# A DeltaNet and MLP-mixer kernel on one core: its steps issued in another order

## The chip, the cores and the metric

The kernel runs on 1 core of one Trainium2 chip. A core has a matrix engine (PE, with its weight loads shown apart as PEld), a vector engine (DVE), a scalar engine (ACT), GpSimd (POOL) and a queue that issues DMAs (SP). Each works through its own instructions strictly in the order in which the program issued them, and waits on semaphores for the others. The metric is device microseconds of one execution.

## The reference, cut to what matters

```python
# q, k, v: (4, 8, 768, 48)    beta: (4, 8, 768)
k_n = k / (np.linalg.norm(k, axis=-1, keepdims=True) + 1e-06)
for t in range(S):                                 # a state of 48x48 per batch and head
    y[:, :, t] = np.einsum('bhd,bhde->bhe', q[:, :, t], state)
    v_old = np.einsum('bhde,bhd->bhe', state, kt)
    state = state + bt * np.einsum('bhd,bhe->bhde', kt, vt - v_old)
x = y.transpose(0, 2, 1, 3).reshape(4, 768, 384)
h = np.maximum(xt @ w_tok1, 0.0) @ w_tok2          # over tokens: xt is x transposed, 768 -> 256 -> 768
u = x + h.transpose(0, 2, 1)
out = u + np.maximum(u @ w_ch1, 0.0) @ w_ch2       # over channels, 384 -> 1536 -> 384
```

The mixer's weights come in as 64-bit floats; everything else is 32-bit.

## The kernel before

**Work and its pieces.** The sequence is cut into 24 units of 128 tokens (6 per batch) and 48 chunks of 64 tokens. The recurrence is done chunk by chunk: each unit first needs small Gram matrices of its keys and queries and the inverse of a triangular matrix, and then a chain of 36 chunk steps carries the state on. After that come the token mixing of each batch and its channel mixing, which is most of the matrix work.

Every piece is a Python generator that issues a few instructions at each step. The letters used below: `k` loads keys and queries of a unit, `v` its values; `p` (`prep`, L528) takes squares and norms of the keys (ACT L539, DVE L542, ACT L547 and L548), transposes keys and queries on PE (L562, L582; copied out by ACT L566, L587) and scales a mask and the keys on DVE or POOL (L574, L592); `c` and `d` (`grams`) make the Gram matrices (PE L511, DVE L517); `t` hands them to `i` (`invert`, L717), which inverts a round of four units (two in the second) on DVE; `f`, `h` and `j` put the inverted blocks together (PE L777, L790, ACT L795, L869 and L818); `r` (`recur`, L903) is one chunk step; `w` rounds a piece of the mixer's weights; `m0` and `m1` are the mixer of batches 0 and 1, whose matmuls need no new data of the recurrence for long stretches and stand wherever the order puts them; `T2`, `T3`, `A`, `F` and `B` are token and channel mixing of batches 2 and 3, done by fast matrix products that trade matmuls for additions on DVE (L1296 in `T3`, L1451 and L1478 in `A`, L1578 in `B`); `x`, `z`, `Y` are matmuls on zeros that keep PE busy.

**What sets the order.** One string lists all 2610 steps, word by word (`p0*5` is five steps of `p0`). A loop calls the generators in that order:

```python
for word in order.split():
    name, _, n = word.partition("*")
    for _ in range(int(n or 1)):
        next(jobs[name])
```

There is no other scheduler: the place of a step in the string is its place in the queue of each engine that it uses, the DMA queue among them. Buffers are waited for as they come free.

**A weight piece** (`round_weights`, L271) is a DMA of 384 KB or 256 KB into one of three buffers named `d64` (L280), two conversions on ACT (L286, L287), a shift on DVE (L289) and an addition on POOL (L293), which reads the buffer last. So a load of one piece cannot start before the POOL addition of the piece three loads earlier is done. The four parts are up to four steps of the string, and may stand far apart.

**A chunk step** `r` has one copy on ACT in its middle: `p_w` is made on PE (L944), ACT copies it to `rw_t` (L950), and PE goes on from it (L958, L959) to the next state. ACT's queue holds those copies among the conversions of weights and all other copies.

**The first round** `i0` is a chain on DVE: a transpose (L731), 14 pairs of a product and a sum on one array (L739, L744), and a transpose back (L753); ACT, DVE and PE take over from it, and the recurrence of units 0 to 3 waits for them.

Of the kernel before, what the change touches and what calls it, by code (L numbers as in the profile page):

```python
# [23 lines left out]
def kernel(  # L24
# [41 lines left out]
    B, H, S, D = q.shape  # L66
# [117 lines left out]
    t11 = const.tile([128, NB, HB], FP32, name="t11")  # L184
# [17 lines left out]
    w1 = const.tile([128, NCH, DTOK], FP32, name="w1")  # L202
    w2 = const.tile([128, NDH, S], FP32, name="w2")
# [407 lines left out]
    t16 = spare[:, cuts[1] : cuts[2]].rearrange("s (q t b) -> s q t b", q=2, t=QB)  # L611
# [1173 lines left out]
    p6*2 t5 j1 t5*2 r1*2 j1 j2 p7 h3*2 r1*3 p6*3 i1*2 r2*5 k8*2 f3*2 w9 k9*3 j1*2
    v2*2 i1*3 j2*2 r2*2 f3 i1*2 p6*3 w16 v2 w16*3 r2*2 h3 r2 i1 d6 r3*5 i1*2 w9*3
    v2 d6 h3 v2 w0 h3*2 r3 h3 d6*2 w0 d6 j3 c6*5 r3*4 w0 j2 w0 p8*2 j2 r4 p8 r4*4
    k9*3 j3*2 r4*2 i1*2 w24 i1*2 p7*7 r4 c7 r4 r5*5 k10 p9 k10 p9 c7 r4 c7*3 i1
    w5*2 p7 r5*2 w24*3 r5*3 j3*2 i1 r6*4 w26 v3*5 p9 k11 r6 d7*5 w26*3 p8*3 t6*2
    r6*2 w5*2 p8*4 v4*2 t6 i1 r6*3 h5*2 h4*2 k10*2 f4*3 c8*2 k10 p10 w28*2 c8*2 r7  # L1790
    c8 r7*3 d8*4 p9 d8 w28 h4*5 p9 t6 r7*2 j4 w28 p9*3 r7*2 p9 w7 d9 w7 v4*2 f5*2
    w27*2 w7*2 d9*4 c9*2 f5 c9*3 t7*2 t8 r7*2 t7*2 j4*2 v4 p10*2 h5 r8*3 w29 t8*3
    w29 w27*2 r8*2 w29*2 q3 w29 j4*2 r8 w22*4 t9*3 r8*3 p9 r9 p10 r9*3 t9 v5 h5*3
    j5 i2 r9 w4*2 r8 h5 i2*5 w4 i2 w19*2 k10 w32 p10*2 w32 v7 k12 m0*2 k11 k12 q0
    v5*3 p10*2 r9*2 j5*2 k11*3 i2*2 r9 w4 i2 j5 i2*3 p10 v5 r9*2 d10*3 r10 v7*2 j5
    i2*2 r10*4 w12 i2 k12 i2*2 m0 w32 k11 k12 w32 r10*2 m0 p11 k12*4 w19 p11 r10
    c10 r10 c10 r10 w33 d10*2 q2 Y r11*4 v7 r11*3 w19 c10 q1 w30 c10 r11 k12*2
    i2*3 r11 v6*4 i2*5 m0*3 i2*5 q5 i2 m0 p11*4 c10 p11 m0 p11*2 m0*2 k12*2 w12
    m0*3 v6 f6*3 w12 d11 c11*2 d11*2 c11 w33 c11 d11*2 j6 p12 w12 m0 w33 w30*3
    p12*2 f7*3 j6*2 m0 c11 j7 f6 f8 w27*2 f8 j7 f8 w15 f7 m0 w29 w33 w29 j7 r12*4  # L1800
    w31 j8 p11 t10*3 r12 Y r12 f9 j8 f9 w21 p12 r12 f8 r13*2 w15*2 r12 w15 r13*3
    w31*3 Y r13*2 w33 j8 w21 m0 r13 q4 p12*4 r13*2 m0*2 r14 c12 f9 j9 r14*2 w21
    t10 w20*2 v7 r14*2 c12*2 w33 c12 r14 v8 c12*2 r14*2 w25*2 j9 r14 r15 v8 w21
    r14 r15 w25 r15*3 w25 k13*4 w20 k13*4 p13 k13*2 w20 v8*3 m0*2 p13 w25 p13 m0
    r15 p13 r15 p13 w27 w25 k13*2 j9 m0*4 p13 f9 w23 t12*3 p13 t12 w25 r15*3 c13*6
    w23 k14*7 r16*5 m0 p13 m0*3 w23*4 k14 r16*2 t11 t13*2 j9*2 t11*3 w33 p14 r16*2
    p14*2 w31 m0*3 w31 m0 w31 m0 w23 r17*2 r16 t13 r17 t13 r17*2 p14*2 m0*2 p14 i3
    k14*4 i3*3 k15 v9*2 m0*3 v10 i3*5 k15 i3 r17 k15*2 p14 k15*3 m0 v10*2 i3 k15*2
    m0*2 k15*2 i3*4 r17*4 k15 i3*2 p14 m0*2 i3*6 m0*4 r18 i3 r18*2 v9*3 r18*2 i3*8
    m0*10 v10*2 m0 r18 c14*4 r18*2 m0*2 f10 c14 f10*2 f12*2 p15*3 m0*4 r18 r19 r18  # L1810
    r19*3 j10 f10 j10*2 f12 p15 f11*4 f12 r19 c14 r19 v11 p15*3 k16*7 j11 m0*2
    r19*4 j11 j12 r20*3 k16*2 r20 m0 r20 k16*3 v11 m0 j11 r20*2 v11*2 p15 c15*2
    p10 r20*2 c15 r20 c15*3 f13*3 p16 r21*5 m0 r21*2 p16*4 k17*7 p16 j12*2 p16 k17
    r21*3 m0*3 r22 c16 r22*3 k17*4 v11 r22 c16*4 r22*2 m0 r22 t14 p17 f13 c16 t14
    j13*2 t14 r22 r23 t15*2 t16 r23*2 r22 r23 m0*3 r23 t15*2 r23 p17*5 t16 p17 j13
    t16*2 m0*3 t14 c17*5 r23*2 c17 t17*2 m0*8 p17 t17*2 i4*3 v12 m0 k18 v15*2 i4
    m0 i4 m0 i4*3 m0 i4 k18*2 j13 p16 m0*2 j13 i4*4 m0 v12*3 k18*4 v12 k18 r24*2
    r23 v13*5 m0 k18*4 v15*2 i4*2 m0*2 p18 i4 p18 r24*3 m0 r24 i4 m0 p18*2 r25*4
    p18 k19*8 i4 m1 r25 i4 m1*4 i4 m1 v14 i4*2 v14 i4*8 r24*3 r25*2 m1 v14 i4*2
    v14*2 p18*2 r25 m1*2 p19 m1*5 k19*4 p19 f14*2 r25*5 c18*5 f14 c18 p18 r26*3  # L1820
# [62 lines left out]
```

## Time and profile before

| | |
|---|---|
| median of 3 runs | 624.91 us (623.32 to 626.13) |
| profiled execution: span | 619.7 us, 20909 instructions |
| around the span, median less span | 5.2 us |
| busy: PE | 590.3 us (95%), 8733 instructions |
| busy: DVE | 469.1 us (76%) |
| busy: ACT | 256.9 us (41%) |
| busy: POOL | 109.9 us (18%) |

The profiled execution is listed by its span only; its own time is taken as the median, so that 5.2 us of the time lie outside the span. The span runs from the first instruction to the last. Busy time of PE counts matmuls at whatever clock was granted to the engine at the time, so that a matmul takes twice as long in a stretch of half clock. The profile has for each line of the program, engine and shape the mean time of one instruction, and for each idle stretch of an engine what ended it. A DVE or POOL row that runs into the next one (starts plus times overlap by some hundredths of a microsecond) is read as back to back.

### The profile page before, as it was taken

The numbers are of one execution on the slowest core, as the hardware profiler recorded it, in microseconds if no ns is written. First come the engines' busy times: TensorE is split into PE (matmuls) and PEld (weight loads), VectorE is DVE, ScalarE is ACT, GpSimd is POOL, SyncE is SP. The second block draws the span as 40 slices with busy tenths as digits, with TensorE's granted clock in tenths as the row PEclk, the third lists the DMA queues.
The fourth block names the chain that finished last, engine by engine and source line by source line (L and its number), as shares of the span: only waits on it lengthen the run. The fifth ranks groups of instructions, "written<-read, shape, count | busy, mean of one in ns | idle before, by whom it ended". The sixth has DMA issues, their size and how long they took to land.

```text
span 619.7 us, 20909 instructions
## 1 busy us (share of the span) xinstructions
PE 590.3 (95%) x8733; PEld 515.9 (83%) x8733; DVE 469.1 (76%) x1160; ACT 256.9 (41%) x682; POOL 109.9 (18%) x150
## 2 busy tenths in 40 slices
PE   8588997999999999999999999999999999999998
PEld 5467875667898988877889888897699999999997
DVE  5987875986889855697566996866888898685874
ACT  8758796448521344223551215415352331414200
POOL 2348264225311122003020120010000000000000
PEclk9878797999999999999999999999999999999999
DMA  9667567667653254454445443135102012020001
GB/s 219 136 135 169 138 142 185 129 155 179 126 114 72 67 116 83 95 113 99 92 87 126 83 95 83 32 66 140 32 2 39 1 21 47 12 52 13 14 26 51
DMA packets 154605, 55.52 MB, mean 90 GB/s; under 512 B 129648, under 2 KB 148976, under 8 KB 154512
## 3 DMA queue, kind: packets, MB, share of 16 engines
q1 hardware_dynamic: 154512, 54.20, 39.1%
q8 instruction: 68, 1.11, 0.8%
q14 instruction: 25, 0.20, 0.1%
HBM read 41.19 MB, written 11.21 MB: 85 GB/s over the span
## 4 chain that ended last, share of the span: by engine, by line
PE 74%; DVE 9%; DMA 4%; ACT 4%; issue 2%; SPq 1%; POOL 1%; DVEq 0%; POOLq 0%; ACTq 0%
PE p_c L1668 13%; PE p_r L1498 13%; PE p_o L1689 10%; PE p_a L1570 7%; PE p_b L1570 6%; PE p_g L511 3%; DMA d<-in_moe_w_ch_dram 3%; PE p_h L1608 3%; DVE sub L739 2%; PE p L1593 2%; DVE x L744 2%; PE p_k L920 2%; PE p L1223 1%; PE p_h L1238 1%; PE p_y L1034 1%
## 5 line engine op out<-in xcount | busy, mean ns | idle before, releaser
L1668 PE MATMUL p_c<-u_t,wc 128*128 128x256 f32 x432 | 101.6, 386 | 0.5 <-issue 0.5
L1668 PEld LDWEIGHTS p_c<-u_t,wc 128*128 128x128 f32 x432 | 79.6, 190 | 11.9 <-issue 1.1
L1689 PE MATMUL p_o<-wc,r 128*128 128x192 f32 x360 | 64.6, 331 | 0.7 <-DVE xb L1628 0.7
L739 DVE TENSOR_TENSOR sub<-x 128x84 f32<-128x84 f32 (+24 forms) x178 | 58.4, 328 | 7.4 <-DMA x<-n_dram 2.8
L744 DVE TENSOR_TENSOR x<-x,sub 128x84 f32<-128x84 f32 (+24 forms) x178 | 58.2, 327 | 6.1
L1689 PEld LDWEIGHTS p_o<-wc,r 128*128 128x128 f32 x360 | 58.4, 190 | 2.3 <-DVE xb L1628 1.3
L1677 ACT ACTIVATE r<-p_c 128x512 f32<-128x512 f32 x36 | 21.4, 596 | 51.2 <-PE p_c L1668 46.1
L511 PE MATMUL p_g<-kq 48*64 48x128 f32 (+1 forms) x704 | 34.9, 283 | 4.0 <-ACT kq L587 3.3
L517 DVE TENSOR_TENSOR gm<-p_g,mb 128x512 f32<-128x512 f32 x44 | 28.9, 683 | 8.1 <-PE p_g L511 7.5
L484 POOL TENSOR_TENSOR v_st<-v_st,nrm 128x384 f32<-128x384 f32 x12 | 10.3, 856 | 131.9 <-DMA v_st<-in_v_dram 104.4
L574 POOL TENSOR_TENSOR mb<-mask_c,cs 128x512 f32<-128x512 f32 x20 | 21.2, 1062 | 67.8 <-DVE cs L552 36.9
L511 PEld LDWEIGHTS p_g<-kq 48*64 48x64 f32 (+1 forms) x704 | 26.5, 137 | 7.6 <-ACT kq L587 4.3
L293 POOL TENSOR_TENSOR wc<-w_f,d 128x384 uint32<-128x384 uint32 x24 | 24.6, 1029 | 42.8 <-ACT d L287 14.1
L1511 DVE TENSOR_TENSOR kq<-kq,p_r 128x384 f32<-128x384 f32 x40 | 21.0, 551 | 10.7 <-PE p_r L1498 8.8
L1498 PE MATMUL p_r<-t_d,wc 128*128 128x192 f32 x160 | 28.8, 326 | 0.0
L1511 DVE TENSOR_TENSOR gm<-gm,p_r 128x384 f32<-128x384 f32 x40 | 21.1, 551 | 8.1 <-PE p_r L1498 5.8
L400 DVE STREAM_TRANSPOSE kq<-pads 128x512 f32<-128x512 f32 x24 | 25.5, 1108 | 2.0 <-PE p_w L1038 1.6
L1498 PEld LDWEIGHTS p_r<-t_d,wc 128*128 128x128 f32 x160 | 26.5, 190 | 0.0
L1689 PE MATMUL p_o<-wc,s 128*128 128x192 f32 x144 | 25.7, 330 | 0.6 <-DVE xb L1628 0.6
L1498 PE MATMUL p_r<-pads,wc 128*128 128x192 f32 x128 | 25.4, 326 | 0.0
L1628 DVE TENSOR_TENSOR xb<-xb,p_o 128x192 f32<-128x192 f32 x42 | 14.6, 348 | 13.0 <-PE p_o L1689 12.6
L1689 PEld LDWEIGHTS p_o<-wc,s 128*128 128x128 f32 x144 | 23.3, 190 | 1.2 <-DVE xb L1628 0.9
(315 smaller groups left out, 1387.1 us busy)
## 6 DMA issues: line engine op xcount, KB each, us to landing
d<-in_moe_w_ch_dram SPq DMA_DIRECT2D x24, 384.0 KB, 4.2
v_st<-in_v_dram SPq DMA_DIRECT2D x96, 48.0 KB, 2.9
out_dram<-xb SPq DMA_DIRECT2D x23, 192.0 KB, 2.1
kst<-in_k_dram SPq DMA_DIRECT2D x64, 48.0 KB, 2.8
n_dram<-gm SPq DMA_DIRECT2D x72, 32.0 KB, 2.3
pads<-in_k_dram SPq DMA_DIRECT2D x24, 96.0 KB, 2.9
pads<-in_q_dram SPq DMA_DIRECT2D x24, 96.0 KB, 2.7
gm<-w_dram SPq DMA_DIRECT2D x72, 32.0 KB, 2.3
```

The lines of the kernel that those rows point to most:

```text
L293: nc.gpsimd.tensor_tensor(out=dst.bitcast(U32), in0=f, in1=lo, op=ALU.add)
L400: nc.vector.transpose(kq_of[p // 2][:, i, :, p % 2].rearrange("f p (s g) -> f p g s", g=G), rows_of[i].rearrange("s p (g d) -> s p g d", g ...
L511: nc.tensor.matmul(p_g[PAR[i ^ cc ^ swap(u)], p], kqt[f, p, cc, 0], kqt[f, p, cc])
L517: nc.vector.tensor_tensor(out=blocks(gm_of(u))[:, :, cc, D:GW].rearrange("s p (two n) -> s p two n", two=2), in0=p_g, in1=made[u][:, :, cc ...
L739: nc.vector.tensor_tensor(out=tmp, in0=y[:, :, 0:s, s : s + 1].to_broadcast([n, k, s, w]), in1=y[:, :, s : s + 1, s + 1 : m].to_broadcast( ...
L744: nc.vector.tensor_tensor(out=y[:, :, 0:s, s + 1 : m], in0=y[:, :, 0:s, s + 1 : m], in1=tmp, op=ALU.add,)
L1498: nc.tensor.matmul(p[:, i], pieces[q // width][:, at : at + 128], f[f"u{n}"], start=first and i == 0, stop=True, skip_group_check=True,)
L1511: nc.vector.tensor_tensor(out=o, in0=o, in1=p, op=op_of(sign))
L1570: nc.tensor.matmul(p, a[:, i], w[:, i // 2, i % 2], start=first and i == 0, stop=True, skip_group_check=True,)
L1668: nc.tensor.matmul(p_c[:, k], piece_of(wc1, cb, f * 128)[:, f * 128 : (f + 1) * 128], u_t[:, cb], start=(cb == 0), stop=(cb == NCB - 1),)
L1677: nc.scalar.activation(r2[:, m], p_c, ACTF.Relu)
L1689: nc.tensor.matmul(p, a[:, m], wc2[:, m, j], start=(start and i == 0), stop=(i == NM - 1), skip_group_check=True,)
```

## The change

Only the string is replaced. Both strings have the same 2610 steps, each generator's steps come in their own sequence as before, and both kernels issue the same 4437 matmuls and the same instructions on every other engine; only the order in each queue differs. The first two lines of it:

```diff
     order = """
-    w10 x*4 z w10*2 z w1*4 k1*3 z k1*3 z b p1 z p1 k0*6 p0*2 b*2 p1 w2 p0*5 p1*2
-    w10 p0*2 z w3 w2 c0*3 p0 w3*2 d0*2 w3 c0 p1 c0 d0*3 k2*3 v1 p1*2 w18 k2*2 p1*2
...
+    w10*2 k1*4 w1 b x k1*2 x*2 p1*2 x*3 z w1 k0*3 z w1*2 z w10 k0 w10 z k0*2 w2 z
+    p0 p1 b*2 k3 v1 p0*3 p1*2 z p0*5 d0*5 w2 c0 k2*2 v1*2 v0 p1 c0*4 k2 p0 p1*2
...
```

Two rows of queues tell more than the string does. A row is the line, the operation, output<-inputs by tile name, the shape and how many stand in a row.

**Start of the program, POOL.** This is POOL's queue from the transposed first parts (L679) to the first block handed back (L706 `wc_120<-r_124`), which comes after the DVE chain of `i0`. Before:

```order
L293 TENSOR_TENSOR wc_119<-w_f,d_282 128x384
L574 TENSOR_TENSOR mb<-mask_c,cs 128x512
L293 TENSOR_TENSOR wc_119<-w_f,d_403 128x384
L652 MEMSET r_124 128x32x16
L619 MEMSET z_571 128x2304
L592 TENSOR_TENSOR gm<-kst_98,cs 128x8x48
L706 COPY wc_120<-r_124 32x8x32
```

and now, beginning one instruction before the mask of unit 3 (`mb`, L574):

```order
L679 COPY r_124<-gm 32x8x32 x2
L574 TENSOR_TENSOR mb<-mask_c,cs 128x512
L293 TENSOR_TENSOR wc_119<-w_f,d_301 128x384
L592 TENSOR_TENSOR gm<-kst_98,cs 128x8x48
L293 TENSOR_TENSOR wc_119<-w_f,d_459 128x384
L652 MEMSET r_124 128x32x16
L619 MEMSET z_588 128x2304
L457 TENSOR_TENSOR nrm<-nrm,eps 128x8
L460 TENSOR_TENSOR v_st<-v_st,nrm 128x384
L706 COPY wc_120<-r_124 32x8x32
```

Between the mask and L706 there were one weight addition (L293), two memsets and one scaling of keys (L592). Now there are two weight additions and the same scaling, the memsets, and two instructions of `v` (L457, L460); the scaling stands ahead of the second addition instead of behind both memsets.

**Steps r8 and r9, ACT.** This is ACT's queue around the copy `rw_t<-p_w` of chunk step `r8` (the first L950 in each piece) and of `r9` (the last row). L286 and L287 on `d_...` are the conversions of one weight piece. Before:

```order
L950 COPY rw_t<-p_w 128x192
L795 COPY gm<-p_x 16x8x16 x3
L286 ACTIVATE d_1927<-d_1927 128x256
L287 ACTIVATE d_1927<-d_1927 128x256
L972 ACTIVATE xb<-p_y 64x4x48 x2
L795 COPY gm<-p_x 16x8x16
L286 ACTIVATE d_1954<-d_1954 128x384
L287 ACTIVATE d_1954<-d_1954 128x384
L566 COPY kq<-p_t 128x4x128
L286 ACTIVATE d_1960<-d_1960 128x384
L287 ACTIVATE d_1960<-d_1960 128x384
L950 COPY rw_t<-p_w 128x192
```

and now:

```order
L950 COPY rw_t<-p_w 128x192
L547 ACTIVATE nrm<-ksum 128x8
L548 ACTIVATE ksum<-nrm,eps 128x8
L795 COPY gm<-p_x 16x8x16 x3
L286 ACTIVATE d_1783<-d_1783 128x384
L287 ACTIVATE d_1783<-d_1783 128x384
L972 ACTIVATE xb<-p_y 64x4x48 x2
L286 ACTIVATE d_1965<-d_1965 128x256
L287 ACTIVATE d_1965<-d_1965 128x256
L869 COPY zst<-p_z 32x256 x2
L566 COPY kq<-p_t 128x4x128
L950 COPY rw_t<-p_w 128x192
```

Between the two copies stood three weight pieces (`d_1927`, `d_1954`, `d_1960`); now there are two (`d_1783`, `d_1965`). In front of the copy of `r8` stands, counted from the start of the program, the twenty-first piece instead of the twenty-second (its conversions are the rows right ahead of the copy in both kernels), and in front of that of `r9` the twenty-third instead of the twenty-fifth.

**Token mixing of batch 3, DVE.** This is DVE's queue in the stretch where `T3` ends (L1296 `xb<-xb,p_h`, which frees the results `p_h` of PE's L1372) while `A1` prepares the channel mixing of its second half (L1451, L1478). Before:

```order
L1296 TENSOR_TENSOR xb<-xb,p_h 128x2x192 x8
L1578 TENSOR_TENSOR xb<-xb,p_a 128x192 x2
L1296 TENSOR_TENSOR xb<-xb,p_h 128x192 x4
L1478 TENSOR_TENSOR t_d<-pads 128x192 x3
L1478 TENSOR_TENSOR t_d<-t_d,pads 128x192
L1478 TENSOR_TENSOR t_d<-pads 128x192
L1478 TENSOR_TENSOR t_d<-t_d,pads 128x192
L1296 TENSOR_TENSOR xb<-xb,p_h 128x192 x4
L1478 TENSOR_TENSOR pads<-pads 128x192
```

and now:

```order
L1578 TENSOR_TENSOR xb<-xb,p_a 128x192
L1296 TENSOR_TENSOR xb<-xb,p_h 128x2x192 x8
L1451 STREAM_TRANSPOSE r_6709<-xb 128x3x128
L1478 TENSOR_TENSOR t_d<-pads 128x192 x2
L1578 TENSOR_TENSOR xb<-xb,p_a 128x192
L1296 TENSOR_TENSOR xb<-xb,p_h 128x192
L1478 TENSOR_TENSOR t_d<-pads 128x192
L1478 TENSOR_TENSOR t_d<-t_d,pads 128x192
L1478 TENSOR_TENSOR t_d<-pads 128x192
L1478 TENSOR_TENSOR t_d<-t_d,pads 128x192
L1478 TENSOR_TENSOR pads<-pads 128x192
L1478 TENSOR_TENSOR t_d<-pads,t_d 128x192
```

On PE, four matmuls `p_a` (L1570, `B0`) stood between the last `p_h` of this stretch and the first `p_r`. Now they stand ahead of the last `p_h`, and on DVE a transpose (L1451) and eight additions of `A1` (L1478) have moved in front of or between the additions that free `p_h`.

149 lines of the change are left out of this document (81 added, 68 removed).

## The prediction

> **What bounds the kernel now.** I read the page first: the busy shares, the slices and the chain that ended last.
>
> ```profile
> span 619.7 us, 20909 instructions
> PE 590.3 (95%) x8733; PEld 515.9 (83%) x8733; DVE 469.1 (76%) x1160; ACT 256.9 (41%) x682; POOL 109.9 (18%) x150
> PE   8588997999999999999999999999999999999998
> PEclk9878797999999999999999999999999999999999
> PE 74%; DVE 9%; DMA 4%; ACT 4%; issue 2%; SPq 1%; POOL 1%; DVEq 0%; POOLq 0%; ACTq 0%
> ```
>
> PE is the bound, and an order cannot shorten its matmuls. It can only take away PE's idle time and its stretches of reduced clock. Both lie in the first eighth of the slices. A table by stage says how much there is; its columns are the stretch, its length, busy time of PE, PEld, DVE, ACT and POOL, the granted clock, DMA share and GB/s.
>
> ```profile
> 26.73:40.82 14.09, 8.79 (x44) 4.91 (x45) 12.34 (x36) 4.48 (x9) 6.40 (x6) 0.64 0.79 178
> 98.34:112.56 14.22, 10.61 (x158) 7.47 (x158) 8.86 (x30) 6.74 (x18) 4.82 (x6) 0.64 0.68 173
> 115.65:446.00 330.35, 325.11 (x5602) 271.22 (x5603) 247.03 (x633) 122.31 (x353) 57.35 (x75) 1.00 0.45 100
> 446.00:616.80 170.80, 170.56 (x1045) 169.12 (x1043) 132.84 (x294) 48.34 (x102) 0.00 (x0) 1.00 0.11 24
> ```
>
> From 115.65 us on PE idles 330.35 − 325.11 = 5.2 us and then 170.80 − 170.56 = 0.2 us. So a better order can win little there and only lose, while of the first 115 us the two stretches above alone hold 5.3 and 3.6 us of idle PE, at a clock of 0.64. The third view is what PE waited for from 17 to 115 us (total, times, longest):
>
> ```profile
> PE p_t L582 <- DMA pads<-in_q_dram: 5.4, 1, 5.4
> PE p_s L958 <- ACT rw_t L950: 3.5, 5, 2.0
> PE p_g L511 <- ACT kq L587: 3.3, 4, 1.4
> ```
>
> The first is one wait in the first round's chain, the second the copy in the middle of a chunk step. I went on to the chain and the timelines around these two places, then to the end of the token mixing.
>
> **The change, first place: weights on ACT (85 to 113 us).** The chain of waits runs over loads of weight pieces there. The last such piece of it (start, length) and rows of ACT's timeline (in brackets the idle time before and what ended it):
>
> ```profile
> 104.29 7.29 DMA d<-in_moe_w_ch_dram
> 101.02 0.55 ACT L286 ACTIVATE d<-d 128x384 f32<-128x384 f32 x1 [1.93 <-DMA d<-in_moe_w_ch_dram]
> 102.05 0.32 ACT L950 COPY rw_t<-p_w 128x192 f32<-128x192 f32 x1
> 106.94 0.44 ACT L286 ACTIVATE d<-d 128x256 f32<-128x256 f32 x1 [3.88 <-DMA d<-in_moe_w_tok_dram]
> 107.27 0.42 ACT L287 ACTIVATE d<-d 128x256 uint32<-128x256 uint32 x1
> 108.64 0.55 ACT L286 ACTIVATE d<-d 128x384 f32<-128x384 f32 x1
> 109.66 0.59 ACT L566 COPY kq<-p_t 128x512 f32<-128x512 f32 x1
> 111.67 0.56 ACT L286 ACTIVATE d<-d 128x384 f32<-128x384 f32 x1 [1.42 <-DMA d<-in_moe_w_ch_dram]
> 112.56 0.30 ACT L950 COPY rw_t<-p_w 128x192 f32<-128x192 f32 x1
> 112.89 0.36 ACT L869 COPY zst<-p_z 32x256 f32<-32x256 f32 x1
> ```
>
> ACT, which is idle more than half of the time, stands still for 1.93 + 3.88 + 1.42 = 7.23 us because the next instruction in its queue is a conversion whose load has not landed. Behind those conversions stand the copies of `r8` (102.05) and `r9` (112.56), and the next state waits for these. The new order puts one piece fewer ahead of the first and two fewer ahead of the second. The last one ahead of the copy of `r9` is then a load of 256 KB, as the one converted at 106.94 is now. If it lands when that does, the conversions end at 107.27 + 0.42 = 107.69, and after two copies L869 (0.36 each) and one L566 (0.59) the copy of `r9` comes at 109.0, 3.6 us earlier than 112.56. If it lands only as the second piece does now (108.64), the copy comes at 108.64 + 0.44 + 0.42 + 0.72 + 0.59 = 110.8, 1.8 us earlier. I take 3.6, which is also the idle PE time of this stretch (14.22 − 10.61): a load of this size is the nearest row.
>
> Bounds: nothing, if the loads land later by as much as the copies move up. On SP's queue the load of that piece still stands behind L733, the fetch of the second round, and behind one load that is converted after it; and a buffer is free only when the POOL addition three pieces before is done. On the other side 7.4 us, if the low clock of this stretch goes too: 10.61 × (1 − 0.64) = 3.8 more. So −3.6, from 0 to −7.4.
>
> **Second place: the first round (26 to 41 us).** DVE, POOL, ACT and PE timelines, in that order:
>
> ```profile
> 26.73 1.95 DVE L731 STREAM_TRANSPOSE x<-r 128x1024 f32<-128x1024 f32 x1
> 28.93 0.19 DVE L744 TENSOR_TENSOR x<-x,sub 128x28 f32<-128x28 f32 x1
> 36.39 1.06 DVE L744 TENSOR_TENSOR x<-x,sub 128x28 f32<-128x28 f32 x1
> 37.80 0.71 DVE L753 STREAM_TRANSPOSE r<-x 128x512 f32<-128x512 f32 x1
> 41.20 0.54 DVE L542 TENSOR_REDUCE ksum<-ksq 128x8 f32<-128x384 f32 x1
> 46.42 1.29 DVE L592 TENSOR_TENSOR gm<-lent,cs 128x384 f32<-128x384 f32 x1
> 27.75 1.04 POOL L574 TENSOR_TENSOR mb<-mask_c,cs 128x512 f32<-128x512 f32 x1
> 36.38 1.01 POOL L293 TENSOR_TENSOR wc<-w_f,d 128x384 uint32<-128x384 uint32 x1 [7.59 <-issue]
> 41.77 0.21 ACT L547 ACTIVATE nrm<-ksum 128x8 f32<-128x8 f32 x1
> 42.22 0.60 ACT L781 ACTIVATE z<-p_z,sides 128x128 f32<-128x128 f32 x2
> 30.31 1.09 PE L582 MATMUL p_t<-ident,pads 128*128 128x128 f32 x4 [5.38 <-DMA pads<-in_q_dram]
> 40.82 2.06 PE L777 MATMUL p_z<-r,wc 64*64 64x32 f32 x64 [1.05 <-DVE gm L517]
> ```
>
> PE's longest wait, 5.38 us, ends at 30.31. The new order issues that load of queries right behind the keys of the same unit, so the wait should shrink or go. I cost this at 0: what hides it is DVE's chain from 26.73 to L753, without which p_z (40.82) cannot start. Were that cover gone, it would be worth up to 5.4 us, but nothing in the order shortens that chain.
>
> The chain itself gets longer. DVE has one more L542 inside it (0.54), and a scaling of keys L592 that ran at 46.42 now stands ahead of L731; its 1.29 there overlaps a POOL addition, so I take the 0.54 of L542, which passes over as many elements. Together +1.08. L547 with its partner, which stood ahead of L781 on ACT (42.22 − 41.77 = 0.45), goes earlier: −0.45.
>
> Then POOL. At 36.39 a sum L744 of 28 elements took 1.06 us, at 28.93 the same one 0.19; beside it ran a POOL addition, and both ended together. So a POOL instruction that begins in the chain holds up one sum by about 0.87; beside the transpose L731 the POOL mask at 27.75 did no visible harm. Two or three POOL instructions more (L592 and weight additions) now stand in that part of POOL's queue, where it idled for 7.59 us before. I take one more collision, +0.87, since the first of them can still fall beside L731, which lasts 1.95. [...]
>
> The place: 1.08 − 0.45 + 0.87 = +1.5. Bounds: −0.2 if POOL's work finishes beside L731 and even the present collision goes (1.08 − 0.45 − 0.87), +3.2 with three collisions more. The delay runs on through the chain of engines up to 85 us.
>
> **Third place: token mixing of batch 3 (475 to 486 us).** The chain of waits, PE's timeline, and two groups of DVE by form (busy us, mean ns):
>
> ```profile
> 483.85 1.30 PE p_a L1570 x8
> L1451 DVE STREAM_TRANSPOSE r<-xb 128x384 f32<-128x384 f32 x3 | 1.6, 558 | 0.0
> L1478 DVE TENSOR_TENSOR t_d<-pads 128x192 f32<-128x192 f32 x10 | 3.2, 353 | 0.6 <-ACT pads L1472 0.6
> ```
>
> Here DVE keeps up because four matmuls p_a (1.30 us; 4 in the order, 8 records in the trace) stand between the last p_h and the first p_r, and give it time for the last sums. The new order puts them ahead of the last p_h, and a transpose (0.56) and several L1478 (0.35 each) ahead of sums that free p_h. So the first p_r waits for what the 1.30 us covered, less what DVE has done by then: taken +1.0. Bounds: 0, if DVE has the sums done earlier, as the transpose stands before the pass; +2.2, the cover, the transpose and one sum (1.30 + 0.56 + 0.35).
>
> **The sum.** −3.6 + 1.5 + 1.0 = −1.1: a span of 618.6 us. The median of 624.91 is 5.2 above the profiled span of 619.7, which I leave as it is: 623.8 us. The bounds add up to −7.6 and +5.4, or 617.3 and 630.3. All else I cost at nothing: from 115.65 us on mixer matmuls fill PE, and the cover is the 247.03 of 330.35 us that DVE is busy; if that cover goes, DVE is late next.
>
> **The rivals.**
>
> *Faster: the low clock of the third stretch goes.* The clock comes in stretches of 10.24 us:
>
> ```profile
> 58.57:68.81 10.24, 10.24 (x244) 9.24 (x242) 7.96 (x22) 7.35 (x20) 3.84 (x5) 0.50 0.58 130
> 99.53:109.77 10.24, 7.42 (x74) 5.06 (x66) 5.97 (x21) 4.64 (x14) 3.87 (x6) 0.50 0.77 210
> PE p_w L944 <- ACT gm L818: 0.8, 1, 0.8
> ```
>
> With ACT's waits the stretch at 99.53 falls away: −7.4, and the delay of the start is absorbed, since the loads pace 85 to 113 us; with +1.0 late, −6.4, 618.5 us. For it: 7.23 us of ACT's waiting is a large share of that stretch. Against it: the last row, PE's longest wait in the 10.24 us before it, is only 0.8 us, so what brings the low clock isn't plain. [...]
>
> *Faster: the stretch at 58.57 goes.* PE is busy through all of it at 0.50, so up to 5.1 us: with the sum, 618.7. The order moves the start by a microsecond or two, which can shift it, but no term aims at it.
>
> *Slower: POOL in the first round.* Three collisions more (+3.2), and each also holds back the weight addition that frees a buffer, so that loads land later and ACT waits as now (0 for −3.6): with +1.0, +4.2, 629.1 us. For it: the one collision on record; against it: POOL idled 7.59 us ahead of it, so it has room to work in. It decides from two collisions more on, if ACT's gain is below 0.5 us.
>
> *Slower: DVE falls behind late.* PE idles 0.2 us of 170.80 there and DVE works 132.84. If the cover fails at 2.2 us in each of the three passes `A1` to `A3`, +6.6 + 1.5 − 3.6 = +4.5, 629.4.
>
> *The change does nothing on ACT.* Loads stay the pace: +2.5, 627.4 us.
>
> **How the numbers follow.** The forecast 0.33; the last rival 0.11; the clock at 99.53 0.25; that at 58.57 0.08; POOL 0.17; late DVE 0.06. A measurement of this kernel tells about 0.5%, 3.1 us, from no change. Faster: 0.25 + 0.08 and 0.04 from the forecast's own lower tail, 0.37; slower 0.17 + 0.06 = 0.23; the rest, 0.40, within. The likeliest, 623.8, has 620.5 to 627.5 as its own range; over all cases 616.5 to 630.0, a little beyond the fast rivals and up to the sum's upper bound.
>
> **What the profile after would show.** The wait of p_t for the queries gone and p_z no earlier than 40.8; L731 to L753 longer by one L542 and one or two sums of 28 to 112 elements that take about 1 us; ACT's idle time on `d` between 95 and 115 us below 4 us and the copy of `r9` about 4 us sooner after that of `r8`; the dense mixer matmuls beginning some 2 us sooner than 115.65; PE idle 1 us longer between 446 us and the end. A dense start that is sooner by 5 us or more, or clock digits of 9 in the seventh slice, would mean a clock rival; a later one, POOL's. I would be wrong above all if the clock's low stretches fall otherwise, which no order row shows.

## The result, and the profile after

The new order takes 648.71 us (median of 4 runs, 647.85 to 656.07), the old one 624.12: slower, a ratio of 1.041 with a 95% interval of 1.037 to 1.045. The forecast was 623.8 us, in a range of 616.5 to 630.0. The profiled execution took 648.64 us with a span of 646.9, 27.2 more than before. Only 1.7 us lie around its span, so most of the 5.2 that the forecast put around the old span were something else: the execution profiled before was quicker than the median. The forecast does not hang on this, being the old median less 1.1.

The page of the profile after, the lines that answer to those of before:

```profile
span 646.9 us, 20904 instructions
PE 600.7 (93%) x8733; PEld 521.4 (81%) x8733; DVE 469.5 (73%) x1160; ACT 256.8 (40%) x682; POOL 109.8 (17%) x150
PE   8569898799999999799899899999999999999998
PEclk9869998887999999989999899999999999999999
PE 59%; DVE 14%; SPq 9%; ACT 8%; DMA 6%; issue 3%; DVEq 0%; ACTq 0%
```

PE is 10.4 us longer busy with the same matmuls (a lower clock, 0.963 for 0.975 over the span) and idles 16.8 us more (27.2 − 10.4) over the whole span. In the chain that ended last, PE's share falls from 74% to 59%, and SP's queue goes from 1% to 9%. A table by stage, before and then after, from the ACT copy of `r9` to the first matmul of T2 and from there to the last matmul (columns as in the prediction):

```profile
112.60:421.10 308.50, 303.55 (x5316) 258.01 (x5316) 231.41 (x601) 115.91 (x333) 56.82 (x74) 1.00 0.46 100
421.10:616.80 195.70, 194.76 (x1431) 184.71 (x1421) 151.33 (x334) 57.65 (x131) 1.05 (x1) 1.00 0.14 33
```
```profile
112.80:448.60 335.80, 317.58 (x5326) 268.23 (x5319) 241.57 (x614) 118.92 (x343) 57.31 (x74) 0.96 0.43 95
448.60:643.90 195.30, 194.38 (x1393) 183.80 (x1389) 148.36 (x331) 55.43 (x123) 1.70 (x3) 1.00 0.13 30
```

Up to `r9` the two traces stand 0.2 us apart, and from T2 to the end they take the same. The whole loss, 335.80 − 308.50 = 27.3 us, lies in the stretch that the prediction had called covered. PE idles there 18.2 us instead of 5.0, 13.3 more, and is busy 317.58 − 303.55 = 14.0 us longer, since the clock is no longer full (0.96 for 1.00). What PE waited for longest in the new order, and what DVE waited for from 112 to 450 us:

```profile
PE p_g L511 <- ACT kq L587: 13.3, 4, 10.1
PE p_o L1689 <- DVE xb L1628: 5.9, 2, 3.6
```
```profile
DVE xb L1628 <- PE p_o L1689: 19.0, 13, 2.5
DVE ss_t L967 <- PE p_y L959: 8.8, 6, 2.9
DVE sub L739 <- DMA x<-n_dram: 8.6, 3, 4.1
DVE s L1648 <- ACT r L1677: 8.4, 3, 5.9
DVE t L813 <- DMA gm<-w_dram: 5.8, 5, 2.0
```

The wait of 10.1 us is in the start, beside `i0`'s chain. The second row of PE and the third of DVE belong together. Round i4, on SP, DVE and PE of the new order (L1689 is the last product of the mixer `m0`, and L1628 the sum on DVE that takes its result out of `p_o`):

```profile
257.85 2.17 SPq L474 DMA_DIRECT2D v_st<-in_v_dram  x2
260.11 0.55 SPq L391 DMA_DIRECT2D pads<-in_k_dram  x1
260.70 0.43 SPq L686 DMA_DIRECT2D n_dram<-gm  x1
261.23 0.60 SPq L474 DMA_DIRECT2D v_st<-in_v_dram  x1
261.93 1.53 SPq L686 DMA_DIRECT2D n_dram<-gm  x3
...
264.00 0.45 SPq L686 DMA_DIRECT2D n_dram<-gm  x1
266.13 0.34 SPq L733 DMA_DIRECT2D x<-n_dram  x1
```
```profile
266.69 0.35 DVE L1628 TENSOR_TENSOR xb<-xb,p_o 128x192 f32<-128x192 f32 x1
269.76 0.19 DVE L739 TENSOR_TENSOR sub<-x 128x30 f32<-128x30 f32 x1 [2.72 <-DMA x<-n_dram]
...
274.16 0.34 DVE L1628 TENSOR_TENSOR xb<-xb,p_o 128x192 f32<-128x192 f32 x1
```
```profile
274.55 4.21 PE L1689 MATMUL p_o<-wc,s 128*128 128x192 f32 x12 [3.63 <-DVE xb L1628]
```

The parts of the round go to memory by L686 and come back by L733, which needs all of them. Loads for later (L474, L391) now stand among the L686; each issue holds SP for 0.4 to 1.1 us in these rows. DVE reaches the first pair of the chain 2.72 us before the data are there, and the six pairs that stand ahead of the next sum L1628 hold that sum back to 274.16. PE, which needs the `p_o` that the sum frees, waits 3.63 us, and at 273.6, 2.7 us into this wait, a stretch of half clock begins. In the old order 15 L686 stood in a row, L733 followed at 249.71, DVE did not wait, and three pairs stood ahead of the sum:

```profile
238.81 9.68 SPq L686 DMA_DIRECT2D n_dram<-gm  x15
249.71 0.34 SPq L733 DMA_DIRECT2D x<-n_dram  x1
```
```profile
254.60 0.35 DVE L1628 TENSOR_TENSOR xb<-xb,p_o 128x192 f32<-128x192 f32 x1
254.86 0.18 DVE L739 TENSOR_TENSOR sub<-x 128x30 f32<-128x30 f32 x1
...
256.33 0.36 DVE L1628 TENSOR_TENSOR xb<-xb,p_o 128x192 f32<-128x192 f32 x1
```
```profile
256.13 2.11 PE L1689 MATMUL p_o<-wc,s 128*128 128x192 f32 x12
```

The half-clock stretches of the new order behind 112 us, the largest three:

```profile
123.40:133.60 10.20, 9.28 (x111) 6.18 (x102) 8.81 (x24) 2.10 (x6) 1.04 (x1) 0.50 0.43 104
154.20:161.00 6.80, 6.80 (x146) 5.36 (x143) 3.27 (x6) 1.90 (x5) 2.60 (x3) 0.50 0.36 74
273.60:280.40 6.80, 5.85 (x18) 5.85 (x19) 5.22 (x14) 0.52 (x1) 0.46 (x1) 0.50 0.27 61
```

They hold 21.9 us of matmuls, which take half of that at full clock (the 12 of `m0` above 4.21 and 2.11 us): 11 us. With a fourth of 3.4 us at 362.4 it is 12.7 of the 14.0 us by which PE's busy time grew in this stage. The trace of before has none behind 112 us; in other traces of the old order one of 6.8 us follows at 115 (e7) or 116 (e9).

### The profile page after: what moved, and what is told of

Read it like the earlier page. It is cut to its first block, busy times and chain, and to the rows that moved or that the text cites. A ratio compares the mean times of both kernels' runs of the same rounds, so it can differ in the third digit from the quotient of the medians.

```text
span 646.9 us, 20904 instructions
## 1 busy us (share of the span) xinstructions
PE 600.7 (93%) x8733; PEld 521.4 (81%) x8733; DVE 469.5 (73%) x1160; ACT 256.8 (40%) x682; POOL 109.8 (17%) x150
## 4 chain that ended last, share of the span: by engine, by line
PE 59%; DVE 14%; SPq 9%; ACT 8%; DMA 6%; issue 3%; DVEq 0%; ACTq 0%
PE p_r L1498 12%; PE p_o L1689 7%; PE p_a L1570 6%; PE p_b L1570 6%; PE p_c L1668 5%; DVE sub L739 5%; DVE x L744 5%; SPq L686 3%; DMA x<-n_dram 2%; PE p_g L511 2%; SPq L391 2%; PE p_warm L235 2%; SPq L711 2%; SPq L474 1%; PE p L1223 1%
## 5 line engine op out<-in xcount | busy, mean ns | idle before, releaser
L1668 PE MATMUL p_c<-u_t,wc 128*128 128x256 f32 x432 | 103.6, 392 | 0.1
L1668 PEld LDWEIGHTS p_c<-u_t,wc 128*128 128x128 f32 x432 | 81.4, 194 | 12.1 <-issue 0.6
L739 DVE TENSOR_TENSOR sub<-x 128x84 f32<-128x84 f32 (+24 forms) x178 | 59.7, 336 | 15.1 <-DMA x<-n_dram 10.5
L1689 PE MATMUL p_o<-wc,r 128*128 128x192 f32 x360 | 66.9, 338 | 2.3 <-DVE xb L1628 2.3
L744 DVE TENSOR_TENSOR x<-x,sub 128x84 f32<-128x84 f32 (+24 forms) x178 | 61.0, 343 | 6.1
L1689 PEld LDWEIGHTS p_o<-wc,r 128*128 128x128 f32 x360 | 60.4, 195 | 3.7 <-DVE xb L1628 2.7
L511 PE MATMUL p_g<-kq 48*64 48x128 f32 (+1 forms) x704 | 35.9, 289 | 14.3 <-ACT kq L587 13.3
L574 POOL TENSOR_TENSOR mb<-mask_c,cs 128x512 f32<-128x512 f32 x20 | 21.0, 1050 | 118.4 <-DVE cs L552 117.6
L293 POOL TENSOR_TENSOR wc<-w_f,d 128x384 uint32<-128x384 uint32 x24 | 24.6, 1023 | 46.9 <-DVE w_f L289 17.0
L1689 PE MATMUL p_o<-wc,s 128*128 128x192 f32 x144 | 28.0, 349 | 3.6 <-DVE xb L1628 3.6
L1628 DVE TENSOR_TENSOR xb<-xb,p_o 128x192 f32<-128x192 f32 x42 | 14.6, 348 | 19.3 <-PE p_o L1689 19.0
L1689 PEld LDWEIGHTS p_o<-wc,s 128*128 128x128 f32 x144 | 25.0, 202 | 4.3 <-DVE xb L1628 3.9
```

What stands on the lines that cost most here:

```text
L293: nc.gpsimd.tensor_tensor(out=dst.bitcast(U32), in0=f, in1=lo, op=ALU.add)
L511: nc.tensor.matmul(p_g[PAR[i ^ cc ^ swap(u)], p], kqt[f, p, cc, 0], kqt[f, p, cc])
L739: nc.vector.tensor_tensor(out=tmp, in0=y[:, :, 0:s, s : s + 1].to_broadcast([n, k, s, w]), in1=y[:, :, s : s + 1, s + 1 : m].to_broadcast( ...
L744: nc.vector.tensor_tensor(out=y[:, :, 0:s, s + 1 : m], in0=y[:, :, 0:s, s + 1 : m], in1=tmp, op=ALU.add,)
L1668: nc.tensor.matmul(p_c[:, k], piece_of(wc1, cb, f * 128)[:, f * 128 : (f + 1) * 128], u_t[:, cb], start=(cb == 0), stop=(cb == NCB - 1),)
L1689: nc.tensor.matmul(p, a[:, m], wc2[:, m, j], start=(start and i == 0), stop=(i == NM - 1), skip_group_check=True,)
```

## The experiments

Theory Q: the loss arises behind 112 us, where DVE chains of inversion rounds stand in the queue ahead of sums and copies, and their fetch comes late since SP issues other loads first. Theory S: the start puts all else out of step. Theory C: the clock does it by a phase of its own. All orders below are spliced from the two strings; at a seam, steps that were already issued are left out and missing ones are put in. The comparisons are with runs of the old order on the same chip, whose median was 624.0 in the first four, 623.15 in the second, 624.6 in the third and 622.56 in the last three.

**e1_first.** New order up to `i2`'s fetch, old behind it.

```diff
-    w10 x*4 z w10*2 z w1*4 k1*3 z k1*3 z b p1 z p1 k0*6 ...    (old, up to i2)
+    w10*2 k1*4 w1 b x k1*2 x*2 p1*2 x*3 z w1 k0*3 z w1*2 ...   (new, up to i2)
```

> The new order up to the first step of the inversion round i2 (about 107 us), the old order of the remaining steps after it. Theory Q (the loss arises behind 112 us, where DVE chains of the rounds i2, i4 and i5 stand in the queue ahead of sums and copies that PE waits for, and their fetch from memory comes late): the copy of r9 was at 112.6 before and 112.8 after, so this kernel takes 624 us, within 2. Theory S (the start, with its 10.1 us wait of PE, puts everything behind it out of step): at least 636 us.

Measured 631.05 us, 1.011 (1.007 to 1.015): 7 us, more than Q had and less than S. Its trace, of its longest run, shows where they arise: at the seam of the two orders. DVE stands still until a piece of weights that L303 sends to memory at 106.77 has been written, and the sum of the chunk step (L967), for which PE waits, stands behind it:

```profile
110.61 0.36 DVE L318 TENSOR_TENSOR wc<-wc 128x192 f32<-128x192 f32 x1 [4.76 <-DMA wc_dram<-wc]
```
```profile
PE p_k L920 <- DVE ss_t L967: 3.8, 1, 3.8
```

The copy of `r9` was at 119.2, behind a half-clock stretch of 13.7 us. From 85 to 125 us DVE waited 1.5 us for such a write in the old order and not at all in the new one, so that e1 prices its own seam and not the new order ahead of `i2`.

The place of the half-clock stretches in the first 120 us differs from run to run of the same code (the last of the trace of before begins at 99.5 us, while e7 and e9, of the same order up to there, have one at 115 and 116), and one trace does not price this stage to better than about 5 us: the old code reached the end of `i2`'s chain at 131.3 in the profile of before, and between 130.7 and 135.8 in the traces of e3, e5, e7, e9 and e11, which have the same order up to there.

**e2_i2.** Old, new from `i2`'s fetch to `r12`, old.

```diff
-    i2 r9 w4*2 r8 h5 i2*5 w4 i2 w19*2 k10 w32 p10*2 ...   (old, i2 to r12)
+    i2 k12 p10 h5 r8 i2 j5 m0*2 i2*2 r9 w19 w4 Y i2*2 w4 v5 j5 ... (new, less what was issued)
```

> The old order up to the first step of i2, the new order from there to the last step of chunk step r12 (about 107 to 150 us), the old order of the rest. Theory Q: the delay that the trace of after gathers between the copies of r9 and r12 (143.9 to 151.8, less the 0.2 at r9, 7.7 us) comes with this stretch alone: about 631.5 us. Theory S: about 624 us, since the start is the old one.

Measured 627.07 us, 1.005 (1.002 to 1.008). The place costs 3 us, not the 7.7 expected: Q's size is wrong here, though S is excluded too. Part of the 7.7 lies in the trace of before, which was a quick one at this place: its copy of `r12` stood at 143.9, and between 143.2 and 148.3 in the traces of e3, e5, e7, e9 and e11.

**e3_i4.** Old, new from `r22` to the end of `i4`'s chain, old.

```diff
-    t17*2 m0*8 p17 t17*2 i4*3 v12 m0 k18 v15*2 i4 m0 i4 m0 i4*3 m0 i4 ...
+    v12 c17*4 t17*3 m0*3 f13 m0*6 j13 t17 i4 k18 v12 r23 i4*6 m0*4 ...
```

> The old order up to the first step of r22, the new order from there to the last DVE step of round i4, the old order of the rest. Theory Q: the part of the loss that the trace shows between the ends of i3 and i4 (18.7 less 11.8, 6.9 us) comes with it: about 631 us. Theory S: about 624 us. Theory C (stretches of half clock come and go by their own phase, whatever PE waits for): only the 3.6 us of waiting, 628 us.

Measured 631.93 us, 1.014 (1.010 to 1.019): the 7 us of Q and something over. Its trace repeats the picture: L733 at 254.82 instead of 249.71, 2.40 us of waiting on DVE, a wait of 3.41 us on PE, and a half-clock stretch of 3.4 us that begins 0.9 us after the wait's end. Theory C, with 628 us, lies outside the interval.

**e4_sums_first.** The new order with one exchange at i4.

```diff
-    i4*6 m0*4
+    m0*4 i4*6
```

> The new order with one exchange: the first six DVE steps of round i4 behind the four mixer steps m0 that follow them, so that the sums L1628 do not stand behind a chain that waits for its fetch. Theory Q: the wait of 3.6 us goes and with it the half-clock stretch of 6.8 us that begins at 273.6 (half of it, 3.4): about 641.7 us. Theory C: the wait goes and the clock stays, 645 us. Theory S: 648.7 us.

Measured 646.84 us, 1.038 (1.033 to 1.042), against 1.041 for the new order. The expectation failed: PE's wait was 3.39 us instead of 3.63, two sums further on, and half clock came from 274.7. The exchange had only moved the chain: ten pairs now stood in a row ahead of the next sums.

**e5_i4_chain and e6_i4_fetch.** The two halves of e3. e5 takes only the order from the fetch on, which is the first step of `i4` (six pairs ahead of the sum), e6 only puts loads ahead of the fetch.

```diff
 e5
-    i4*3 v12 m0 k18 v15*2 i4 m0 i4 m0 i4*3 m0 i4
+    i4 p16 v13*4 k18 v12 m0 j13 k18 v12 r23 i4*6 m0*4 ...
 e6
-    t17*2 m0*8 p17 t17*2 i4*3 v12 m0 k18 ...
+    k18*3 v12*4 t17*2 m0*8 p17 t17*2 i4*3 m0 ...
```

> The old order up to the fetch of round i4 (L733), the new order from there to the end of i4's chain on DVE, then the old order: the fetch comes as early as before, and six pairs L739 and L744 stand ahead of the second sum L1628 instead of three. The kernel with the whole place (e3) had that sum at 263.08, 7.2 us behind the one before it, of which 2.40 were the wait for the fetch, and PE waited 3.41. Theory Q1 (late fetch and packed chain are both needed): the sum comes about 4 us sooner than in e3, PE does not wait, 624 to 625.5 us. Theory Q2 (the packed chain alone does it): about 631 us.

> The old order with seven loads (three steps of k18 and four of v12) moved ahead of the last two steps of t17, so that they stand ahead of the fetch of round i4 on SP; DVE's and PE's queues stay as they were. Theory Q1: the fetch comes some 4 us later, but only three pairs stand ahead of the second sum; PE waits 1.5 us at the most, 624 to 627 us. Theory Q3 (the late fetch alone does it): PE waits 3 us and more and a stretch of half clock follows, about 631 us.

e6: 628.02 us, 1.007 (1.002 to 1.012). In its trace the fetch is late by a wait of 2.99 us on DVE, and PE waits for the sums:

```profile
PE p_o L1689 <- DVE xb L1628: 3.2, 2, 1.7
```

So the late fetch alone brings waits of PE back, 3.2 us as Q3 had it, but in two pieces, and no half clock follows; the time lies between Q1 and Q3, and its interval tells neither off. e5: 630.2 us, 1.012 (1.007 to 1.016), with runs from 622.8 to 633.9. Its trace, of the run of 622.8, has the second sum at 257.11 and no wait of PE above 0.3 us for a sum, as Q1 had it; its median has not, and speaks for Q2. By the times either half of e3 costs something alone.

**e14_chain_again.** The same kernel as e5, for a second trace.

> The kernel of e5 (old order, i4's chain packed, fetch early) once more, for a second trace. If the chain is early by a margin of less than the fetch varies: in a run of 627 us or more DVE waits for the fetch of i4 and PE for the sum L1628 behind the chain, 1 us or more; in a run of 624 us or less neither. If a slow run shows no wait there, its time is the clock's or another place's.

This run took 624.29 us. DVE did not wait for the fetch, and PE waited 0.4 us for a sum. No longer run of this kernel was caught in a trace, so what makes most of e5's runs longer stays open. Half clock is not it: four of them, from 627.7 to 631.1 us, have a mean granted clock of 0.976 to 0.978, and the run of 622.8 has 0.978.

**e7_from_i5 and e11_i5.** Old up to the end of `i4`'s chain, then new: in e7 to the end, in e11 to the end of `i5`'s chain only.

```diff
-    i5 m1*4 i5 v17*2 r26 i5*2 m1*2 r28 k22*3 i5*4 ...
+    k22 r29 i5 r28 r29*3 i5 r29 r27 r26 r28 i5*5 m1*2 k22*2 p22 ...
```

> The old order up to the end of i4's chain (about 282 us), the new order of everything behind it. In the trace of after the rest of the loss, 27.2 less 18.7, 8.5 us, arises there: 632.5 us. Should the late stage lose only in company with the delays of the stages ahead (loads and sums out of step), 624 to 627 us. The prediction's third place (token mixing of batch 3, +1.0, 0 to 2.2) is in it.

> The old order up to the end of i4's chain, the new order to the end of i5's chain, the old order behind it: from 282 to 359 us. In the trace of e7 DVE waited 4.6 us for the fetch of i5 (2.1 before), PE 2.3 us for a sum behind that chain, and 5.7 of the 8.6 us were lost by the end of i5. Theory Q: 629 us (628 to 630.5). If the loss belongs to the steps from i5 on (recurrence of the last units): 624 to 625 us.

e7: 631.98 us, 1.015 (1.010 to 1.019), 8.8 us, as the trace of after had it. e11: 629.79 us, 1.006 (1.002 to 1.010), 5.2 us. Round i5 has i4's mark, waits of DVE for the fetch and of PE for the sum, and a third one, of PE for a transpose L813, which itself waits for the read-back (L711) of `i4`'s result (e11's trace; in the old order DVE waited for this fetch too, but 2.1 us, and PE 0.4 us for a sum):

```profile
DVE sub L739 <- DMA x<-n_dram: 4.5, 1, 4.5
```
```profile
PE p_o L1689 <- DVE xb L1628: 2.3, 1, 2.3
PE p_z L843 <- DVE t L813: 2.0, 1, 2.0
```

**e8_weights and e12_one_piece.** The prediction's first place. e8: old, new from `r4` to the copy of `r9`, old. e12: the old order, one conversion behind the copy.

```diff
 e12
-    w32 w32 v7 k12 m0*2 k11 k12 q0 v5*3 p10*2 r9*2
+    w32 v7 k12 m0*2 k11 k12 q0 v5*3 p10*2 r9*2 w32
```

> The old order up to the first step of chunk step r4 (about 78 us), the new order from there to the ACT copy of r9 (about 112 us), then the old order: the prediction's first place by itself. In the traces the copy of r9 stood 33.2 us behind that of r5 before (79.4 to 112.6) and 30.4 after (82.4 to 112.8). If that gain lasts: 621.3 us. If the fetch of round i2, which the new order puts behind three more loads, takes it back on DVE: 624 us or up to 627.

> The old order with one exchange on ACT: the conversion of the third weight piece between the copies of r8 and r9 (at 111.67, with a wait of 1.42) goes behind the copy of r9. By the prediction's first place the copy comes at 110.3 to 110.7 instead of 112.56 and the kernel gains about 2 us: 621.2 us. Theory M: DVE is busy without a break with i2's chain from 105.4 us on, and the sum of r9 and the difference of r10 stand in its queue behind a fixed number of pairs (they ran at 114.15 and 116.58), so an earlier copy brings nothing: 623.2 us, within 1.

e12: 624.77 us, 0.998 (0.994 to 1.003): no gain seen, though the interval does not exclude the 2 us expected. The rows decide. The copy of `r9` on ACT did come 1.6 us earlier; `r9`'s sum and `r10`'s difference on DVE did not:

```profile
110.92 0.32 ACT L950 COPY rw_t<-p_w 128x192 f32<-128x192 f32 x1 [0.87 <-PE p_w L944]
```
```profile
114.94 0.35 DVE L967 TENSOR_TENSOR ss_t<-ss_t,p_s 128x192 f32<-128x192 f32 x1
116.84 0.35 DVE L927 TENSOR_TENSOR rw_t<-p_k,v_st 128x192 f32<-128x192 f32 x1
```

In the old order these stood at 114.15 and 116.58. DVE has run `i2`'s pairs without a break since 105.4, and the two stand behind a fixed number of them: theory M. e8: 628.07 us, 1.006 (1.003 to 1.009), 4.9 us and more than was expected of it at the worst. Its copy of `r9` is 10.2 us behind that of `r8` (103.51 to 113.74, 10.5 before); then `i2`'s fetch, behind more loads, makes DVE wait 2.26 us, and `r10`'s difference runs at 120.99.

**e9_late.** Old up to T2, new behind it: the third place.

```diff
-    T2 r33*2 T2 f23 r33 l s l s r33 j23 ...   (old, from T2)
+    T2 s r33 r34 r33*2 r34 f23 s r34*2 s*2 r34 s*2 j23*3 r32 ... (new, with what was missing)
```

> The old order up to the first step of the token mixing T2 (about 421 us), the new order behind it: the prediction's third place by itself, and with it a reordering that touches no inversion round. The prediction had +1.0 (0 to 2.2), so 624 to 626 us; the traces of before and after have 195.7 and 195.3 us from T2's first matmul to the last matmul, so 623 to 624 us. Should any reordering at all cost several microseconds, as the four last runs might suggest: 627 us or more.

Measured 626.75 us, 1.003 (0.999 to 1.007): nothing, or up to 4.4 us. That does not show that a reordering without an inversion round is free. From T2's first matmul to the last its trace takes 199.0 us instead of 195.7, of which 1.4 are a wait of PE for a read-back (`gm<-w_dram`) right behind the seam; PE's wait for the sums of token mixing (L1296) is 0.2 us, as before.

**e10_start.** New up to the end of `i0`, old behind it: the second place.

```diff
-    w10 x*4 z w10*2 z w1*4 k1*3 z ...   (old, up to i0's end)
+    w10*2 k1*4 w1 b x k1*2 x*2 ...      (new, up to i0's end)
```

> The new order up to the end of round i0 (about 42 us), the old order behind it: the prediction's second place by itself, +1.5 (-0.2 to +3.2) there. In the traces i0's chain on DVE ended at 41.1 instead of 37.4. If that runs on to the end: 627.5 us. If the loads of weights pace what follows and take it up: 624 us. The whole first stage (e1) cost 7 us; what this run leaves of them belongs to the steps from i0 to i2.

Measured 627.07 us, 1.002 (0.999 to 1.006). In its trace `i0`'s chain ends 4.5 us later than in that of before (41.92 to 37.43), and the last matmul 3.2 us later; the interval holds no change and 3.8 us. It has the long wait of PE at the start (9.8 us for the copy L587), so theory S, by which that puts 12 us and more on everything behind it, is excluded.

**e13_repair and e15_repair_i2.** The new order with the suspected causes taken away: loads behind the fetch and pairs spread among the sums, in e13 at i4 and i5, in e15 at i2 (there, two pairs behind `r10`'s difference).

```diff
 e13
-    i4 k18 v12 r23 i4*6 m0*4 k18 i4*2 k18 i4 ...
+    i4 v13*3 k18 v12 k18 v12 r23 i4*2 m0 i4 m0 i4 m0 i4*2 m0 ...
-    t21*3 m1 k22*3 m1*3 k22 r29 i5 ... i5*5 m1*2
+    t21*3 i5 m1 k22*3 m1*3 k22 r29 ... i5 m1 i5*2 m1 i5*2
 e15
-    t9*4 k11 j4*3 k12 j4 p10 f5 v5 h5*2 p10 i2
+    t9*4 j4*4 p10 f5 h5*2 p10 i2 k11 k12 v5
```

> The new order with two things taken away: five loads (v13, k18, v12) go behind the fetch of i4 and the fetch of i5 goes ahead of four steps of loads (k22); and the first DVE pairs of i4 and i5 stand singly or in twos between the mixer's sums instead of six and five in a row. Theory Q: the waits of PE of 3.6 and 2.3 us go and with them the half-clock stretches of 6.8 and 3.4 us behind them (5.1 us of time): 637.7 us, 635 to 640. If these two were only companions of the loss: 645 us or more.

> The new order with three loads (k11, k12, v5) moved behind the fetch of round i2 and the last two pairs of i2 ahead of the difference L927 of r10 moved behind it. Theory Q: that difference, at 121.57 in the new order and 116.58 in the old, comes about 3.4 us sooner (1.7 for the loads, 0.85 a pair): 645.3 us; if the half-clock stretch of 10.2 us at 123.4 goes with it, 640 us. If the start's delay sets the time of r10, no change: 648.7 us.

e13: 643.38 us, 1.033 (1.028 to 1.039), against 1.041 (1.037 to 1.045): some 5 us come back, half of what was expected, with intervals that just overlap. At i4 the long wait and the half clock are gone; what PE waited for from 255 to 295 us is now:

```profile
PE p_s L1052 <- ACT rw_t L1043: 1.3, 1, 1.3
PE p_y L959 <- ACT rw_t L950: 0.4, 1, 0.4
```

Against the trace of before, the delay grew by 0.9 us from the sum L967 of `r23` to the end of i4's chain (11.7 to 12.6), where it had grown by 6.3 (12.4 to 18.7). At i5 nothing came back: 6.5 us against 5.8, and a wait of 2.31 us for a sum turned up later in its chain. e15: 648.65 us, 1.042 (1.037 to 1.046), no gain. From the copy of `r9` to that of `r10` it takes 7.6 us instead of 10.0, as meant, but its trace had more half clock around it.

## Why the prediction was wrong

The step that failed is the sentence "All else I cost at nothing". It named the cover, "the 247.03 of 330.35 us that DVE is busy", and that DVE would be late next. It even said that an order can there "only lose", and put no price on it. What the runs show in its place is 27.3 us in that stretch: 13.3 of idle PE and 14.0 of longer matmuls. The 5.2 us of idle PE were the work of an order in which fetches, chains and sums fit closely. DVE's free time is an average; at i4 the sum had to run within some 4 us of the one before it (255.85 to the start of PE's wait at 260.1 in e3), and the chain and its fetch stood ahead. The rows of SP and DVE around L733 would have shown it, and the difference of the two orders there was in hand: the prediction names no place behind 113 and ahead of 475 us.

Three runs of places behind 112 us measure 3.1 (e2), 7.9 (e3) and 8.8 (e7), 19.8 of the 24.6 us of the whole. From `r12` to `r22` no run was made; the traces drift apart there from 8.0 us (copy of `r12`) to 11.8 (end of i3's chain). For i4 the mechanism is shown by putting it in (e3) and by taking it out (e13); for i2 and i5 only the place is.

- *First place, −3.6, 0 to −7.4.* The reading of ACT was right in kind: the wait for loads between `r8` and `r9` fell from 5.30 to 4.03, and `r9` came 9.4 us behind `r8` instead of 10.5 (103.42 to 112.77). That is 1.2 us and not 3.6, since the last load was converted at 110.73 and not at 106.94: the bound "if the loads land later" came near. The term was wrong also because ACT was not what set the next state: DVE was, as the rows of e12 show. Row of the profile missed: DVE's, which is busy from 105.41 on.
- *Second place, +1.5, −0.2 to +3.2.* In the traces +3.6 at the end of `i0`'s chain, beyond the bound, and +2.5 in e10's time, which its interval does not tell from nothing. The chain itself took 11.3 us instead of 10.7: one L542 (0.54) and one more held-up pair, 0.35 instead of the 0.87 assumed. What was missed is its start, 29.77 for 26.73: up to it DVE works 0.9 us more and idles 2.2 us more, for squares on ACT and Gram matrices on PE. PE's wait for the queries went, as forecast, but one of 10.1 us for a later copy took its place. Of the four POOL instructions, two fell beside L731 (1.94 us, 1.95 before) and two beside pairs. Beside those two, one product and one sum took 0.35 and 0.8 us longer than their like (0.54 for 0.19 us at 31.75, beside L592 from 31.41; 1.06 for 0.27 at 37.03, beside L293 from 36.95). The three collisions more of the prediction's bound were too many; one more came, as its sum had it.
- *Third place, +1.0, 0 to 2.2.* Not seen: 195.7 and 195.3 us from T2 on, and no wait of PE for `p_r` in either trace. e9 cannot tell 1.0 us from nothing.
- *The rivals.* The slower ones had the right kind of event (DVE behind late, a fetch behind other work) at the wrong places: POOL at the start and `A1` to `A3`. The two clock rivals got in the trace of after what they asked for, and it did not make the kernel faster. These are the two stretches of half clock of the prediction, after:

```profile
58.57:68.81 10.24, 9.54 (x326) 8.43 (x329) 9.06 (x26) 9.52 (x24) 5.15 (x6) 1.00 0.64 155
99.53:109.77 10.24, 8.45 (x186) 6.28 (x187) 4.91 (x14) 6.15 (x18) 5.32 (x7) 0.83 0.84 220
```

The first is gone and of the second 3.4 us are left. From the end of `i0`'s chain to the copy of `r9` the new order makes up 3.4 us, which with the 3.6 lost at the start gives the 0.2 by which the traces stand apart. That the two cancel is chance: the place of these stretches differs from run to run. The sign that the prediction named for being wrong, low clock that falls otherwise, came true for about half of the loss, but behind 112 us.

Behind 112 us each stretch of half clock of the new order came right behind idle time of PE. These are the 3.4 us ahead of each of the four half-clock stretches there, in the new order:

```profile
120.03:123.44 3.41, 1.48 (x66) 1.12 (x64) 3.34 (x8) 1.26 (x3) 1.04 (x1) 1.00 0.70 169
150.75:154.16 3.41, 1.85 (x60) 1.52 (x61) 1.53 (x6) 3.28 (x12) 0.38 (x1) 1.00 0.85 255
270.22:273.63 3.41, 0.70 (x5) 0.40 (x3) 3.10 (x10) 0.00 (x0) 1.34 (x2) 1.00 0.54 93
358.96:362.38 3.42, 1.12 (x21) 1.00 (x14) 3.15 (x11) 0.52 (x1) 0.00 (x0) 1.00 0.29 60
```

PE is busy for 0.21 to 0.54 of them. Cut into pieces of 3.41 us, the length of the shortest stretch, on the same grid, this stage has no other piece at full clock below 0.69, and the trace of before has none below 0.82. At i4 the idle time is one wait, and without it in e13 no half clock came. At 123.4 and 154.2 it is several short waits, 1.43 and 0.9 us the longest; the one of 1.43 is for the late difference of `r10` (L927, at 121.57), behind i2's pairs. So the traces do not show the phase of its own of theory C there. No limit is shown: in e4 a piece in which PE was busy 1.66 of 3.41 us (from 322.45) was followed by full clock, and no run was made to test it. Nor does the length of one wait tell when the clock falls: it fell 2.7 us into the wait of 3.63 us here, 0.9 us behind the end of the one of 3.41 in e3, and at 123.4 and 154.2 behind waits of 1.43 and 0.9 us at the longest.

Open is what at i2 and i5 carries the loss beside the causes that e13 and e15 took away, what makes most of e5's runs long, and what the order from `r12` to `r22` costs.

## What to carry to other kernels

In an order whose queues fit closely, low idle time on the bound engine is what can be lost, not only what can be won: look at each place where a fetch waits for many small writes, and count what stands ahead of it on the DMA queue and behind it on the engine that consumes it. A wait that ends last on one engine is worth only what the next engine in the chain leaves of it; before it is priced, read whether that one is busy without a break. No version tried here beat the old order; e12 equals it within its noise. A splice of two orders can also cost time at its seam, as e1's did: read its trace before its time is put down to the part that was moved.

## What the runs showed of the hardware

In the trace of after the stretches of half clock lasted 3.4, 6.8, 10.2 and 13.7 us, in that of before 10.2 each. In the new order each one behind 112 us began right behind 3.4 us in which PE was busy 0.21 to 0.54 of the time, whether by one wait or by several short ones. Where the stretches lie in the first 120 us changes from run to run of the same code: the last of the trace of before begins at 99.5 us, while e7 and e9, of the same order up to there, have one at 115 and 116. The end of one chain, `i2`'s, lay between 130.7 and 135.8 in traces of the same order up to there, how much of that by the clock is not shown. An L686, L474 or L391 holds SP's queue for 0.4 to 1.1 us in the rows here: the seven loads that e6 put ahead of a fetch took 3.9 us of the queue (1.34 and 2.58), and the fetch came at 257.09 instead of 249.71, in a run that was already some 2.5 us late at that place. Beside a POOL addition or scaling (L293, L592) one product or sum of `i0`'s pairs on DVE took 0.35 to 0.87 us longer than its like: 1.06 us for 0.19 before, 0.54 for 0.19 and 1.06 for 0.27 after.
